# A fixed bank for each kind of transform piece, and a fixed step parity: one change to an FFT filter with a feed-forward layer behind it

## The chip, the cores and the metric

The kernel runs on one core of a Trainium2 chip. A core has five engines with a queue each: TensorE (PE: matmuls, which write to PSUM), VectorE (DVE), ScalarE (ACT), GpSimd (POOL) and SyncE (SP); the last two only issue DMAs here. PSUM is the memory that matmuls write to; this kernel uses it in banks of 128 x 512 float32 values. The metric is the device time of one execution in microseconds (us). The median of the kernel before is 810.01 us over three runs (808.7 to 810.15).

## The reference

```python
def _attn_ref(x, filt_r, filt_i):
    X = np.fft.rfft(x, axis=1)                     # x: (8, 3008, 256)
    F = (filt_r + 1j * filt_i)[None, :, :]         # 1505 frequencies x 256
    y = np.fft.irfft(X * F, n=x.shape[1], axis=1)
    return y.astype(np.float32)

def _moe_ref(x, w_in, w_out, alpha):               # x: (24064, 256), w_in: (256, 2048)
    h = x @ w_in
    g = np.maximum(h, 0.0) + alpha * np.minimum(h, 0.0)
    return (g @ w_out).astype(np.float32)          # w_out: (2048, 256)
```

The second function takes the result of the first, with its 8 sequences laid end to end. Inputs and output are float32.

## The kernel before

**The transform.** A sequence of 3008 = 47 x 64 points is transformed as 47-point transforms, a twiddled 64-point stage, a product with the filter, and the same way back, all as matmuls in float16. For each sequence ("batch", index b = 0 to 7; batch three of the change's name is b = 2) there are four kinds of pieces, each of which fills one PSUM bank and is then read out:

- A (piece_a, line 158; 16 per batch): one 512-column matmul with the 47-point matrix; ScalarE copies it to asb. After every fourth, save_a stores a chunk to memory; turn_a loads all back in another order, as at.
- B (piece_b, line 180; 12): two 256-column matmuls, the forward products. VectorE reads the bank twice: line 188 multiplies by the swapped filter (ww), line 189 by the filter (uu). GpSimd moves the halves of ww across partitions by DMA (sw). piece_s (line 194) adds sw to uu later.
- C (piece_c, line 199; 12): the inverse 64-point stage, two 256-column matmuls (four for b = 1); ScalarE copies it to v. turn_c stores v and loads it back as zt.
- D (piece_d, line 226; 16): four 94-column matmuls, the inverse 47-point stage; ScalarE copies it to yT, the input of the layers.

Batch 0 is done ahead by a class of its own (First), whose transposes (T and piece_t, lines 266 and 303) and D pieces partly reach into the first 47 steps of the main loop; VectorE copies some of them out.

**The layers.** Tokens go through in blocks of 512 (one in twelve has 384). A block has 16 steps. In step j the first layer makes 128 hidden features (up, line 409: two 512-column matmuls); after every odd j ScalarE copies the two halves of a double bank (hps) to gtb (line 420), and VectorE makes the PReLU of it (lines 423 and 424). In the same step the second layer of the block before does its share (down, line 427: four 256-column matmuls; three after a 384-token block). After j = 7 and j = 15 (10 and 15 after a 384-token block) ScalarE copies a finished output to osb (line 438), which SP stores.

**The order.** There are 768 steps. The program is in the order in which it is written out: in each step first the transform pieces that plan (lines 442 to 485) puts there, in the order in which they were put, then up, then down. Each engine goes through its queue in that order. plan_fft gives for b of 3 and over, with p = 96 (b - 1): A at p - 68 + int(2.4 i), B at p + 5 + {0, 4, 10, 14, 20, 24, 30, 34, 40, 44, 50, 54}, the add 8 steps after B, C 12 after B, and D at p + 91, 92, 93, 94, 95, 97, 99 ... 117. So B, the add and C are on odd steps, A on steps of both parities, D from the fifth piece on odd steps. A of batch b + 1 runs in the same steps as B and C of batch b, D of batch b together with B and the first C of b + 1. For b = 2, A is at 66, 68 ... 96, B at 109, 113, 117, 121, 127 ..., C 12 later, D at 187 on. For b = 1, A is at 16 to 31, B at 40, 43 ... 73, C 6 steps after B and ahead of the B of its step, and D at 92 to 96, 98, 100 ... 118.

**The banks.** Of eight banks, four are hps (two double banks), two op (second layer), and two belong to the pool psF, from which A, B, C and D take theirs (bank, line 142; for some pieces of batch 0 a half of hps). A piece's first matmul waits until the earlier piece in that bank has been read. Which of the two banks a piece gets is settled when the program is built.

Of the kernel before, what the change touches and what calls it, by code (L numbers as in the profile page):

```python
# [11 lines left out]
FP32 = mybir.dt.float32  # L12
# [52 lines left out]
def kernel(  # L65
# [27 lines left out]
    p_osb = ctx.enter_context(tc.tile_pool(name="p_osb", bufs=3))  # L93
    psH = ctx.enter_context(tc.tile_pool(name="psH", bufs=2, space=bass.MemoryType.PSUM))
    psO = ctx.enter_context(tc.tile_pool(name="psO", bufs=2, space=bass.MemoryType.PSUM))
    psF = ctx.enter_context(tc.tile_pool(name="psF", bufs=2, space=bass.MemoryType.PSUM))
    dram = ctx.enter_context(tc.tile_pool(name="dram", bufs=1, space=bass.MemoryType.DRAM))
    a_dram = dram.tile([NB, 96, NH, D], FP16, name="a_dram")
    v_dram = dram.tile([NB, 96, NH, D], FP16, name="v_dram")
# [21 lines left out]
    def xrow(b, h, c):  # L121
        return bass.AP(tensor=x.tensor, offset=x.offset + (b * NFFT + NH * h + 8 * c) * D,
                       ap=[[N2 * D, N1], [1, 8 * D]])

    def load_x(b, c):
        xs = p_x.tile([2 * N1, 8 * D], FP16, name="xs")
        for h in range(2):
            nc.gpsimd.dma_start(out=xs[h * N1 : h * N1 + N1], in_=xrow(b, h, c))  # L128
        return xs
# [9 lines left out]
            in_=bass.AP(tensor=src.tensor, offset=src.offset + (N1 - ka) * D,  # L139
                        ap=[[47 * D, 32], [-D, n], [1, D]]))  # L140

    def bank(wide=False):
        if wide:
            return psH.tile([128, 2, 512], FP32, name="hps")[:, 0]
        return psF.tile([128, 512], FP32, name="psF")


    class Fft:
        def __init__(self, b):
            self.b = b  # L150
            self.base = (b % 2) * NFFT
            self.px, self.uw = {}, {}

        def start_a(self):
            self.asb = p_fft.tile([96, NH, D], FP16, name="asb")
            self.at = p_fft.tile([128, NK1, D], FP16, name="at")

        def piece_a(self, i, evict, wide=False):
            if i == 0:
                self.start_a()  # L160
            xs = xc[(self.b, i // 4)]
            ps = bank(wide)
            o = (i % 4) * 512
            nc.tensor.matmul(ps[0:96], wf1_s, xs[:, o : o + 512], start=True, stop=True)  # L164
            evict(self.asb[:, 2 * i : 2 * i + 2].rearrange("p a d -> p (a d)"), ps[0:96])
# [12 lines left out]
                        in_=a_dram[self.b, r + ka : r + kb].rearrange("k s d -> s k d"))  # L178

        def piece_b(self, kp):  # L180
            px = bank().rearrange("p (k d) -> p k d", k=2)
            for kh in range(2):
                k1 = 2 * kp + kh
                nc.tensor.matmul(px[:, kh], twf_s[:, k1], self.at[:, k1], start=True, stop=True)  # L184
            uu = p_uw.tile([128, 2, D], FP16, name="uu", bufs=4)
            ww = p_uw.tile([128, 2, D], FP16, name="ww")
            sw = p_uw.tile([128, 2, D], FP16, name="sw")
            nc.vector.tensor_mul(ww, px, filts_s[:, 2 * kp : 2 * kp + 2])  # L188
            nc.vector.tensor_mul(uu, px, filt_s[:, 2 * kp : 2 * kp + 2])  # L189
            for o in (0, 64):  # L190
                nc.gpsimd.dma_start(out=sw[o : o + 64], in_=ww[64 - o : 128 - o])  # L191
            self.uw[kp] = uu, sw
# [6 lines left out]
        def piece_c(self, kp, evict, pv=None):  # L199
            if kp == 0:  # L200
                self.v = p_fft.tile([128, NK1, D], FP16, name="v")
                self.zt = p_fft.tile([96, NH, D], FP16, name="zt")
            us = self.uw.pop(kp)
            if pv is None:
                pv = bank().rearrange("p (k d) -> p k d", k=2)
            for kh in range(2):
                k1 = 2 * kp + kh
                for u in us:
                    nc.tensor.matmul(pv[:, kh], twi_s[:, k1], u[:, kh], start=u is us[0], stop=u is us[-1])  # L209
            evict(self.v[:, 2 * kp : 2 * kp + 2], pv)  # L210
# [14 lines left out]

        def piece_d(self, i, evict, wide=False):
            g, dh, mh = i // 4, (i // 2) % 2, i % 2
            pd = bank(wide)
            ps = pd[:, 0 : 8 * N1].rearrange("p (m x) -> p m x", m=4)
            for m in range(4):  # L230
                nc.tensor.matmul(ps[:, m], self.zt[:, 8 * g + 4 * mh + m, dh * 128 : dh * 128 + 128],  # L231
                                 wi3_s, start=True, stop=True)
            t0 = self.base + g * 752
            evict(yT[:, dh, t0 : t0 + 752].rearrange("p (x m) -> p x m", m=8)[:, :, 4 * mh : 4 * mh + 4],
                  ps.rearrange("p m x -> p x m"))
# [208 lines left out]
    def put(step, fn, *args):  # L444
        plan.setdefault(step, []).append((fn, args))

    def plan_fft(b, a0, ga, ta, b0, gap, add, lag, d0, quarters, x_at):
        f = Fft(b)
        for i in range(16):
            put(int(a0 + ga * i), f.piece_a, i, on_act)  # L450
        for c in range(4):
            put(int(a0 + ga * (4 * c + 3)), f.save_a, c)
            if b + 1 < NB:
                put(x_at[c],
                    lambda b=b, c=c: xc.update({(b + 1, c): load_x(b + 1, c)}))
        for q in range(quarters):
            w = NK1 // quarters
            put(ta, f.turn_a, nc.sync, w * q, w * q + w)
        bs = [b0 + (2 * int(gap * kp / 2) if add else int(gap * kp)) for kp in range(12)]
        for kp in range(12):  # L460
            put(bs[kp], f.piece_b, kp)
            if add:
                put(bs[kp] + add, f.piece_s, kp)
            put(bs[kp] + lag, f.piece_c, kp, on_act)
        for q in range(4):
            put(bs[3 * q + 2] + lag + 1, f.turn_c, q)
        for i in range(16):
            put(d0 + min(i, 4) + 2 * max(i - 4, 0), f.piece_d, i, on_act)

    for g, t0, d0, gap, evs in ((1, 0, 6, 1, both), (2, 17, 25, 2, (on_dve,)), (3, 32, 40, 2, (on_act,))):  # L470
        for i in range(4):
# [6 lines left out]
    for i in range(4):  # L478
        put(17 + 3 * i, neg, 6 * i, 6 * i + 6)
    put(29, lambda: nc.gpsimd.dma_start(out=filt_s[64:128], in_=filt_s[0:64]))  # L480
    plan_fft(1, 16, 1, 32, 40, 3, 0, 6, 92, 4, (20, 24, 74, 75))
    plan_fft(2, 66, 2, 97, 109, 4.5, 8, 12, 187, 4, (110, 114, 118, 122))
    for b in range(3, NB):
        p = 96 * (b - 1)
        plan_fft(b, p - 68, 2.4, p - 27, p + 5, 5, 8, 12, p + 91, 1, (p + 6, p + 10, p + 16, p + 20))
# [46 lines left out]
```

## Time and profile before

| | us |
|---|---|
| median of three runs | 810.01 |
| profiled execution, first to last instruction (span) | 805.5 |
| TensorE matmuls busy | 781.5 (97%) |
| VectorE busy | 647.0 (80%) |
| ScalarE busy | 599.1 (74%) |
| A: 112 matmuls of 512 columns, of b = 1 to 7 | 43.1 |
| D: 504 matmuls of 94 columns into psF | 41.9 |
| B: 168 matmuls of 256 columns, of b = 1 to 7 | 32.1 |
| ScalarE copy of A, mean | 0.591 |
| ScalarE copy of C, mean | 0.597 |
| ScalarE copy of D, mean | 0.485 |
| ScalarE copy of 128x1024 to gtb, mean | 1.022 |
| VectorE reads of B, mean each | 0.684 and 0.682 |

The page gives no time for the profiled execution beyond its span. In lines of the profile, out<-in are names of the program (psF is any piece's bank), a bracket at the end of a line of the timeline is the idle time of that engine before the instruction and what ended it, and in the view of waits the three numbers are the sum in us, how many, and the longest. Matmuls overlap, and their ends are modelled: two in a row start closer together than either lasts, so the distance of their starts is the measure of TensorE's pace.

### The profile page before, as it was taken

The numbers are of one execution on the slowest core, as the hardware profiler recorded it, in microseconds if no ns is written. First come the engines' busy times: TensorE is split into PE (matmuls) and PEld (weight loads), VectorE is DVE, ScalarE is ACT, GpSimd is POOL, SyncE is SP. The second block draws the span as 40 slices with busy tenths as digits, with TensorE's granted clock in tenths as the row PEclk, the third lists the DMA queues.
The fourth block names the chain that finished last, engine by engine and source line by source line (L and its number), as shares of the span: only waits on it lengthen the run. The fifth ranks groups of instructions, "written<-read, shape, count | busy, mean of one in ns | idle before, by whom it ended". The sixth has DMA issues, their size and how long they took to land.

```text
span 805.5 us, 16163 instructions
## 1 busy us (share of the span) xinstructions
PE 781.5 (97%) x5980; PEld 538.6 (67%) x5980; DVE 647.0 (80%) x1449; ACT 599.1 (74%) x836; POOL 140.4 (17%) x269
## 2 busy tenths in 40 slices
PE   6999999999999999999999999999999999999997
PEld 5756666666666666766667666766666666776665
DVE  4797985899879897798878888798877999777773
ACT  3788677878778777877868877787877867696663
POOL 7410330232004220131102321032200222000000
PEclk9999999999999999999999999999999999999999
DMA  9977457674756446574484543854465233511111
GB/s 187 199 146 207 106 133 176 185 153 120 166 135 125 110 128 149 138 142 112 112 200 99 113 126 104 211 110 112 114 160 141 53 97 85 134 40 34 41 40 53
DMA packets 94247, 100.59 MB, mean 125 GB/s; under 512 B 11320, under 2 KB 81992, under 8 KB 94040
## 3 DMA queue, kind: packets, MB, share of 16 engines
q1 hardware_dynamic: 79512, 68.80, 32.3%
q0 software_dynamic: 14656, 30.75, 20.1%
q8 instruction: 47, 0.77, 0.4%
q14 instruction: 32, 0.26, 0.1%
HBM read 56.26 MB, written 46.66 MB: 128 GB/s over the span
## 4 chain that ended last, share of the span: by engine, by line
PE 74%; DVE 12%; ACT 7%; issue 3%; DMA 3%; SPq 1%; POOL 0%; ACTq 0%; DVEq 0%; POOLq 0%
PE op L433 32%; PE hps L414 31%; ACT gtb L420 4%; DVE m L423 4%; DVE gtb L424 3%; PE psF L209 3%; PE psF L164 2%; DVE ww L188 2%; DVE uu L189 2%; PE psF L231 2%; PE psF L184 1%; ACT asb L238 1%; DMA xs<-in_x_dram 1%; DMA v_dram<-v 1%; ACT osb L438 1%
## 5 line engine op out<-in xcount | busy, mean ns | idle before, releaser
L420 ACT ACTIVATE gtb<-hps 128x1024 f16<-128x1024 f32 (+1 forms) x384 | 385.4, 1004 | 111.2 <-PE hps L414 110.6
L433 PE MATMUL op<-wout_s,gtb 128*128 128x256 f16 x3008 | 451.1, 272 | 0.6 <-DVE gtb L424 0.6
L414 PE MATMUL hps<-yT,win_s 128*128 128x512 f16 (+1 forms) x1536 | 449.1, 374 | 0.4 <-ACT gtb L420 0.2
L433 PEld LDWEIGHTS <-gtb 128*128 128x128 f16 x3008 | 293.3, 98 | 189.5 <-DVE gtb L424 0.9
L423 DVE TENSOR_SCALAR m<-gtb,alm_s 128x512 f16<-128x512 f16 (+1 forms) x768 | 237.7, 351 | 108.1 <-ACT gtb L420 107.3
L424 DVE TENSOR_TENSOR gtb<-gtb,m 128x1024 f16<-128x1024 f16 (+1 forms) x384 | 261.6, 681 | 24.3 <-PE hps L414 0.5
L191 POOL DMA_DIRECT2D sw<-ww x168 | 87.7, 527 | 503.1 <-DVE ww L188 494.1
L414 PEld LDWEIGHTS <-win_s 128*128 128x128 f16 x1536 | 146.1, 98 | 31.1 <-issue 3.1
L238 ACT ACTIVATE yT<-psF 128x376 f16<-128x376 f32 x120 | 58.2, 485 | 25.4 <-PE psF L231 25.1
L238 ACT ACTIVATE asb<-psF 96x512 f16<-96x512 f32 x112 | 66.1, 591 | 12.4 <-PE psF L164 12.0
L238 ACT ACTIVATE v<-psF 128x512 f16<-128x512 f32 x84 | 50.2, 597 | 29.3 <-PE psF L209 28.9
L438 ACT ACTIVATE osb<-op 128x512 f32<-128x512 f32 x96 | 56.3, 586 | 6.1 <-issue 3.2
L188 DVE TENSOR_TENSOR ww<-psF,filts_s 128x512 f16<-128x512 f32 x84 | 57.4, 684 | 0.1
L189 DVE TENSOR_TENSOR uu<-psF,filt_s 128x512 f16<-128x512 f32 x84 | 57.2, 682 | 0.0
L164 PE MATMUL psF<-xs,wf_s 94*96 94x512 f16 x112 | 43.1, 385 | 1.7 <-ACT v L238 1.0
L231 PE MATMUL psF<-wi_s,zt 96*128 96x94 f16 x504 | 41.9, 204 | 2.5 <-DMA zt<-v_dram 1.6
L231 PEld LDWEIGHTS <-zt 96*128 96x128 f16 x512 | 35.4, 97 | 7.3 <-DMA zt<-v_dram 1.9
L128 POOL DMA_DIRECT2D xs<-in_x_dram x64 | 34.8, 555 | 25.6 <-PE psF L164 13.3
L209 PE MATMUL psF<-uu,twi_s 128*128 128x256 f16 x168 | 33.7, 274 | 4.9 <-DVE uu L189 4.5
L184 PE MATMUL psF<-at,twf_s 128*128 128x256 f16 x168 | 32.1, 272 | 0.2
L196 DVE TENSOR_TENSOR uu<-uu,sw 128x512 f16<-128x512 f16 x72 | 30.1, 418 | 0.0
L209 PEld LDWEIGHTS <-twi_s 128*128 128x128 f16 x192 | 16.7, 98 | 12.8 <-DVE uu L189 10.2
(57 smaller groups left out, 191.3 us busy)
## 6 DMA issues: line engine op xcount, KB each, us to landing
out_dram<-osb SPq DMA_DIRECT2D x128, 128.0 KB
xs<-in_x_dram POOLq DMA_DIRECT2D x64, 188.0 KB, 4.4
a_dram<-asb SPq DMA_DIRECT2D x28, 384.0 KB
sw<-ww POOLq DMA_DIRECT2D x168, 64.0 KB, 2.1
v_dram<-v SPq DMA_DIRECT2D x112, 96.0 KB
zt<-v_dram SPq DMA_DIRECT2D x28, 384.0 KB
at<-a_dram SPq DMA_DIRECT2D x20, 384.0 KB
at<-a_dram SPq DMA_DIRECT2D x32, 96.0 KB
```

Of the source, the lines that this page charges most:

```text
L188: nc.vector.tensor_mul(ww, px, filts_s[:, 2 * kp : 2 * kp + 2])
L189: nc.vector.tensor_mul(uu, px, filt_s[:, 2 * kp : 2 * kp + 2])
L191: nc.gpsimd.dma_start(out=sw[o : o + 64], in_=ww[64 - o : 128 - o])
L209: nc.tensor.matmul(pv[:, kh], twi_s[:, k1], u[:, kh], start=u is us[0], stop=u is us[-1])
L231: nc.tensor.matmul(ps[:, m], self.zt[:, 8 * g + 4 * mh + m, dh * 128 : dh * 128 + 128], wi3_s, start=True, stop=True)
L238: nc.scalar.activation(o, i, AF.Copy)
L414: nc.tensor.matmul(self.hps[:, j % 2, 0:tn], win_s[:, kt, j * 128 : (j + 1) * 128], yT[:, kt, self.t0 : self.t0 + tn], start=(kt == 0), st ...
L420: nc.scalar.activation(g[:, :, 0:tn], self.hps[:, :, 0:tn], AF.Copy)
L423: nc.vector.tensor_scalar(m[:, i, 0:tn], g[:, i, 0:tn], 0.0, a, OP.min, OP.mult)
L424: nc.vector.tensor_add(g[:, :, 0:tn], g[:, :, 0:tn], m[:, :, 0:tn])
L433: nc.tensor.matmul(self.op[:, si % 2], self.gts[k][:, 128 * si : 128 * si + 128], wout_s[:, k], start=(k == 0), stop=(k == 15))
L438: nc.scalar.activation(osb[:, 0:m], self.op[:, 0:m], AF.Copy)
```

## The change

The pool psF becomes two pools of one bank each, and bank takes a number. For b of 2 and over, A, C and D always take bank 0 and B bank 1. For b = 0 and 1 a counter flips at each call, and the pieces take the banks strictly in turn. In the plan, A of b of 2 and over goes to even steps only: for b of 3 and over the pieces at offsets 7, 9, 19, 21, 31 and 33 come one step earlier, and so does the first save_a; b = 2 already was on even steps, and for b of 3 and over the others stay. D of b of 2 and over has its pieces 4 to 15 one step later, on even steps (p + 96, 98 ... 118). For b = 1 the plan is as it was. In the diff, the four changed calls of bank are, in order, those of A, B, C and D.

```diff
-    psF = ctx.enter_context(tc.tile_pool(name="psF", bufs=2, space=bass.MemoryType.PSUM))
+    psF = [ctx.enter_context(tc.tile_pool(name=f"psF{i}", bufs=1, space=bass.MemoryType.PSUM)) for i in range(2)]
...
-    def bank(wide=False):
+    side = [0]
+
+    def bank(wide=False, n=None):
         if wide:
             return psH.tile([128, 2, 512], FP32, name="hps")[:, 0]
-        return psF.tile([128, 512], FP32, name="psF")
+        if n is None:
+            side[0] ^= 1
+            n = side[0]
+        return psF[n].tile([128, 512], FP32, name="psF")
...
             self.px, self.uw = {}, {}
+            self.n = (0, 1) if b > 1 else (None, None)
...
-            ps = bank(wide)
+            ps = bank(wide, self.n[0])
...
-            px = bank().rearrange("p (k d) -> p k d", k=2)
+            px = bank(False, self.n[1]).rearrange("p (k d) -> p k d", k=2)
...
-                pv = bank().rearrange("p (k d) -> p k d", k=2)
+                pv = bank(False, self.n[0]).rearrange("p (k d) -> p k d", k=2)
...
-            pd = bank(wide)
+            pd = bank(wide, self.n[0])
...
+        at_a = (lambda i: int(a0 + ga * i)) if b == 1 else (lambda i: 2 * int((a0 + ga * i) / 2))
         for i in range(16):
-            put(int(a0 + ga * i), f.piece_a, i, on_act)
+            put(at_a(i), f.piece_a, i, on_act)
         for c in range(4):
-            put(int(a0 + ga * (4 * c + 3)), f.save_a, c)
+            put(at_a(4 * c + 3), f.save_a, c)
...
+        at_d = 4 if b == 1 else 3
...
-            put(d0 + min(i, 4) + 2 * max(i - 4, 0), f.piece_d, i, on_act)
+            put(d0 + min(i, at_d) + 2 * max(i - at_d, 0), f.piece_d, i, on_act)
```

## The prediction

> **What bounds the kernel now.** I read the page first, then the view of who waited for whom, then the timeline around the places that the change touches.
>
> ```profile
> span 805.5 us, 16163 instructions
> PE 781.5 (97%) x5980; PEld 538.6 (67%) x5980; DVE 647.0 (80%) x1449; ACT 599.1 (74%) x836; POOL 140.4 (17%) x269
> PEclk9999999999999999999999999999999999999999
> PE 74%; DVE 12%; ACT 7%; issue 3%; DMA 3%; SPq 1%; POOL 0%; ACTq 0%; DVEq 0%; POOLq 0%
> ```
>
> TensorE is the bound and its clock is full throughout. In the timeline its matmuls start back to back: 216 ns apart at 512 columns, 109 at 256, 41 at 94; a step without transform pieces takes 2 x 216 + 4 x 109 = 868 ns. So what counts is lost starts: the distance of two starts less the streaming time of the first. Added up over the timeline from 90 us on they are 15.9 us. So I count what each bank change adds or removes there. No other engine is near 100% over a long stretch, and a wait of TensorE moves everything behind it.
>
> ```profile
> PE psF L209 <- DVE uu L189: 4.5, 15, 0.8
> PE psF L231 <- DMA zt<-v_dram: 1.6, 1, 1.6
> PE psF L164 <- ACT v L238: 1.0, 2, 0.5
> ```
>
> Inverse pieces (C, line 209) wait 15 times for line 189, VectorE's second read of a forward product (B): the C piece got the bank that B still held. That is what the change takes away. (This view counts idle time from modelled ends, so it reads lower than the lost starts.)
>
> ```profile
> 203.03 0.60 ACT L238 ACTIVATE v<-psF 128x512 f16<-128x512 f32 x1 [0.45 <-PE psF L209]
> ...
> 203.68 0.38 PE L164 MATMUL psF<-xs,wf_s 94*96 94x512 f16 x1 [0.47 <-ACT v L238]
> ```
>
> This row gives the price of sharing a bank with ScalarE: the next user starts 0.05 us after the copy's end.
>
> **Steps 209 to 637 and later (b = 3 to 7): C.** Lost starts of C, and of A behind C in the same step, are in the timeline 2.20, 2.87, 2.20, 2.86 and 0.57 us for b = 3 to 7: 10.7 us (this includes 0.04 us on each first-layer matmul behind a C-A pair). All vanish. But C now shares bank 0 with A and D, and these now sit on even steps, just ahead of C's odd ones. The case is in the trace:
>
> ```profile
> 277.45 1.02 ACT L420 ACTIVATE gtb<-hps 128x1024 f16<-128x1024 f32 x1 [0.81 <-PE hps L414]
> ...
> 277.69 0.38 PE L164 MATMUL psF<-xs,wf_s 94*96 94x512 f16 x1
> ...
> 278.37 0.59 ACT L438 ACTIVATE osb<-op 128x512 f32<-128x512 f32 x1
> 278.54 0.68 DVE L189 TENSOR_TENSOR uu<-psF,filt_s 128x512 f16<-128x512 f32 x1
> 278.85 0.59 ACT L238 ACTIVATE asb<-psF 96x512 f16<-96x512 f32 x1
> ...
> 279.28 0.39 PE L209 MATMUL psF<-uu,twi_s 128*128 128x256 f16 x2 [0.34 <-DVE uu L189]
> ```
>
> Step 232 runs A at 277.69; ScalarE copies it at 278.85 to 279.44, since the gtb copy of the odd step before and an output copy stand ahead. C of step 233 could start at 277.69 + 1.09 = 278.78, waits for VectorE until 279.28 (0.50), and on A's bank would wait until 279.49: 0.71. Without an output copy (steps 222 and 223) A's copy ends at 267.97, C could start at 267.80: 0.22, where VectorE cost 0.34. Behind D the copy is shorter: 0.16, or 0.63 behind an output copy (0.43 where that is the half-size one, after the 384-token block). From the new plan, with p = 96(b-1), C of p+17 and p+21 come behind D (the first with an output copy), p+31, 37, 47, 61 behind A, p+41 and 57 behind A with an output copy, and p+27, 51, 67, 71 behind an empty step. Sum per batch: 0.63 + 0.16 + 4 x 0.22 + 2 x 0.71 = 3.07 (2.87 for b = 4, 6); b = 7 has only D, 0.79. In all 12.7 for 10.7: +2.0. A behind C waits nothing: C's copy ends 1.05 us after C's start, the next step comes at 1.09, and this margin is thin.
>
> **D of b = 2 to 7.** Its first four steps stay consecutive, and now on one bank: in the trace the third would wait 0.17 us for the copy of the second (b = 2, 4, 6) or 0.11 (3, 5, 7): +0.84. The 12 others (4 matmuls and a copy each, no DMA) move one step later; the first block that reads them starts ten steps after, so nothing waits.
>
> **C of b = 2** (steps 121 to 169): now 1.52 of lost starts; then C behind A at 125, 133, 139, 143, 151, 157 for 0.22 each and 129, 161 with an output copy for 0.71: 2.73. +1.2.
>
> **Moved A** (six per batch b = 3 to 7: one matmul and one copy each, one step earlier, and with the fourth the save_a store of chunk 0): on the SP queue no other issue stands between old and new step, POOL gets none; nothing.
>
> **Batches b = 0 and 1: strict turns.** Before, one pool had both banks, and a piece got the one that came free first:
>
> ```profile
> 50.83 0.38 PE L164 MATMUL psF<-xs,wf_s 94*96 94x512 f16 x1
> ...
> 51.64 0.68 DVE L241 CAST zt<-psF 96x512 f16<-96x512 f32 x1
> ```
>
> A of step 18 started at 50.83, while the bank of step 17's transpose was read until 52.32: it took the other. The new code flips a side at each call, so it must take this one: 52.36, a wait of 1.53. By going on like this in the timeline, letting VectorE run on while TensorE waits: step 20 waits 0.05 (VectorE has caught up), step 22 1.00, step 28 0.97, step 32 0.26; waits of 0.28, 0.28 and 0.11 (steps 19, 21, 29) go. Steps 16 to 32: +3.1.
>
> From step 40 on, counting flips, B of b = 1 always has side 0 and C side 1, and A of b = 2 (bank 0, steps 66 to 96) runs into B:
>
> ```profile
> 111.91 0.38 PE L184 MATMUL psF<-at,twf_s 128*128 128x256 f16 x2
> ...
> 112.80 0.38 PE L164 MATMUL psF<-xs,wf_s 94*96 94x512 f16 x1 [0.51 <-ACT v L238]
> ...
> 114.16 0.68 DVE L189 TENSOR_TENSOR uu<-psF,filt_s 128x512 f16<-128x512 f32 x1
> ```
>
> In step 70 A would follow B at 112.13, waits now until 112.80 (0.67), and on B's bank until 114.89: 2.75. Likewise A of step 66 waits for B of 64 (read until 107.88; A at 106.91): 1.02; A of 68 for B of 67: 0.65 (B's reads end 1.70 us after its start when VectorE is free, the next A comes 1.09 after); A of 74: 0.66; C of 79 behind A of 78: 0.23. B of 73 keeps its 0.28. Steps 66 to 80: 1.02 + 0.65 + 2.08 + 0.66 + 0.23 = +4.6. VectorE's reads are what is late there: a step-69 copy and three VectorE instructions stand ahead of B's, so the wait moves on whole.
>
> Steps 92 to 118 (D of b = 1 in turns, A of b = 2 on bank 0, B of b = 2 on bank 1): D at 93, 95, 98 behind A's copies 0.23, 0.37, 0.10; B at 109, 113, 117 behind D's copies 0.48, 0.55, 0.17; a wait of 0.18 at 112 goes: +1.7. The 1.8 us that D's first piece waits for its zt load stays: that chain starts from C of step 79 and moves with it.
>
> **Sum**: 2.0 + 0.8 + 1.2 + 3.1 + 4.6 + 1.7 = +13.4 us, on the profiled span 805.5: 818.9. The page gives no time around the span; the median of the timed runs is 810.0, 4.5 above it, and I keep that: 823.4.
>
> **The clock.** Longest new wait: 2.75 us. The present one of 1.8 us at 136.64 left the granted clock at 1.00 from 134 to 140 us, so I put nothing. The Trainium skill (TensorE: Matmul & The Clock Gate, "A second HAM failure mode: psum-queue depth-cycling") says that waiting on PSUM banks between groups of matmuls can make the clock swing between half and full. This trace, with its 15.9 us of lost starts at a full clock, does not bear it out; if it held, the sum would be that of rival 3.
>
> **Bounds.** The waits on ScalarE are read from copies that are in the trace; what is not there is how far an engine catches up while TensorE waits. If VectorE doesn't catch up, steps 18 to 32 cost what their present lags say, 1.53 + 1.29 + 1.07 + 0.54 + 0.97 + 0.35 + 0.26 less the 0.67 that goes, 5.3 for 3.1, and A of 68 0.90 for 0.65: with the thin margin of A behind C (some 35 pairs, at most 0.05 us each), up to +18, 828. If it catches up more, steps 16 to 80 cost half: +9.5, 819.5.
>
> **Rivals.** (1) The early part does not come: the first two batches' pieces still find the bank that is free, as before. For it: before did so; against it: two pools of one bank each and a counter leave no choice. Then 2.0 + 0.8 + 1.2 = +4.0: 814.0. (2) Faster: ScalarE's copies are not late. If A's copy began within 0.45 us of A's start (1.09 less 0.59 less 0.05) C would never wait; then the 12.2 us of b = 2 to 7 go, the ScalarE waits of steps 79 to 118 and of D don't come, and the VectorE waits 3.1 + 4.4 stay: -4.7, 805.3. Against it: on even steps of the 512-token blocks A's copies begin 0.68 us after A, 1.16 with an output copy, behind the gtb copy, whose place doesn't change. (3) The clock drops after the 2.75 us wait. The trace's own half-clock stretch is its start: 128-column matmuls 107 ns apart from 2.67 to 5.4 us, 56 after. One such stretch of 2.7 us loses 1.4 us: 824.8. (4) The two effects cancel, within 0.2% (1.6 us, about what these runs can tell from no change).
>
> **How the numbers follow.** Forecast as summed, with its bounds 819.5 to 828: 0.75. (1) 0.11, (3) 0.03: slower together 0.89. (2) 0.08. (4) 0.03. Range: 812.5 to 828 takes in the forecast and (1) and (3), leaving out about one in ten.
>
> **What would show it** (line numbers of the kernel before). Right: the row of line 209 waiting for DVE uu goes, line 209 waiting for ACT asb (and yT) comes, some 40 times, 0.2 or 0.7 us each; line 164 waits for DVE uu and zt, a few times, 1 to 2.75 us, before 120 us; TensorE's starts from 209 on lose about 13.5 us in place of 10.7. Wrong: no wait of line 164 over 1 us before 120 us (rival 1), or line 209 starting 1.09 us after A throughout (rival 2).

## The result and the profile after

The changed kernel takes 823.06 us (median of four runs, 822.31 to 824.32); the kernel before, beside it on the same chip, takes 809.36 (808.09 to 810.15, four runs). The ratio is 1.0178 (95% interval 1.016 to 1.0196): slower by 13.7 us, where the prediction said 823.4 in a range of 812.5 to 828. The profiled execution of the changed kernel took 823.26 us with a span of 821.5, so 1.8 us lie around the span.

The page of the changed kernel: span, engines, the clock that TensorE was granted, and the shares of the chain that ended last.

```profile
span 821.5 us, 16161 instructions
PE 786.9 (96%) x5980; PEld 541.5 (66%) x5980; DVE 647.8 (79%) x1449; ACT 595.1 (72%) x836; POOL 139.9 (17%) x269
...
PEclk9999999999999999999999999999999999999999
...
PE 80%; ACT 9%; DVE 5%; issue 2%; DMA 2%; POOL 0%; SPq 0%; ACTq 0%; DVEq 0%; POOLq 0%
```

TensorE does the same 5980 matmuls. In the chain, VectorE's share has gone from 12% to 5% and ScalarE's from 7% to 9%: the waits for VectorE's reads went, and waits for ScalarE's copies came. The view of waits (sum in us, how many, the longest) says at which pieces. Lines are moved by 6 against the kernel before: 170 is A, 190 B, 195 VectorE's second read of B, 215 C, 237 D, 244 a ScalarE copy, 247 a VectorE copy.

```profile
PE psF L170 <- DVE uu L195: 4.5, 4, 2.6
PE psF L215 <- ACT asb L244: 4.4, 8, 0.6
...
PE psF L215 <- ACT yT L244: 2.3, 5, 0.5
PE psF L170 <- DVE zt L247: 1.8, 2, 1.0
PE psF L237 <- DVE yT L247: 1.4, 1, 1.4
```

The row of C waiting for uu is gone. In its place C waits for ScalarE's copies of A (asb) and of D (yT), and four A of b = 2 (the row with uu) wait for VectorE: the banks of the early steps. This view counts only what the modelled ends leave over; counted as lost starts, as in the prediction, C waits 42 times from 140 us on, for 16.2 us. Here are two of them in the timeline, at step 229 (without an output copy) and step 233 (with one):

```profile
286.21 1.02 ACT L426 ACTIVATE gtb<-hps 128x1024 f16<-128x1024 f32 x1 [0.67 <-PE hps L420]
...
286.45 0.38 PE L170 MATMUL psF<-xs,wf_s 94*96 94x512 f16 x1
286.96 0.68 DVE L195 TENSOR_TENSOR uu<-psF,filt_s 128x512 f16<-128x512 f32 x1
287.13 0.58 ACT L244 ACTIVATE asb<-psF 96x512 f16<-96x512 f32 x1
...
287.77 0.38 PE L215 MATMUL psF<-uu,twi_s 128*128 128x256 f16 x2
```

```profile
290.81 0.38 PE L170 MATMUL psF<-xs,wf_s 94*96 94x512 f16 x1
291.49 0.59 ACT L444 ACTIVATE osb<-op 128x512 f32<-128x512 f32 x1
...
291.97 0.59 ACT L244 ACTIVATE asb<-psF 96x512 f16<-96x512 f32 x1
292.61 0.38 PE L215 MATMUL psF<-uu,twi_s 128*128 128x256 f16 x2 [0.55 <-ACT asb L244]
```

In the first, C could have started 1.09 us after A, at 287.54; it starts at 287.77, 0.05 after ScalarE has emptied A's bank, and 0.23 is lost. In the second the output copy stands ahead of A's copy: 0.72 lost.

**Where the 13.7 us are.** For each step the timeline gives the start of its first-layer matmul; the difference to the same step of the kernel before, and where that difference grows, is the account of the change. The profiled execution of the changed kernel is one column; a second profiled execution of the same kernel, from the experiments (span 820.9), is the other. The main loop's first step comes at another time in each execution, 0.9 and 1.4 us later here than in the profile before, and that is left out.

| steps | predicted | first profile | second |
|---|---|---|---|
| 0 to 16 | 0 | 0.72 | 0.72 |
| 16 to 32 | 3.1 | 2.75 | 2.74 |
| 33 to 64 | 0 | -0.33 | -0.23 |
| 64 to 80 | 4.6 | 6.24 | 4.85 |
| 81 to 92, with the zt wait of step 92 | 0 | -0.51 | -0.48 |
| 93 to 118 | 1.7 | 1.73 | 1.75 |
| 118 to 169: C of b = 2 | 1.2 | 1.26 | 1.27 |
| 169 to 767: C and D, b = 3 to 7, and D of b = 2 | 2.8 | 3.23 | 3.32 |
| sum | 13.4 | 15.1 | 13.9 |

The first profile has 1.67 us that the second lacks: TensorE's clock. (The row of steps 64 to 80 differs by 1.4, since B of step 73 then no longer waits its 0.28.) At step 70 A waits for B's bank, 2.76 us by starts, and then:

```profile
117.75 0.38 PE L190 MATMUL psF<-at,twf_s 128*128 128x256 f16 x2
120.73 0.45 PE L170 MATMUL psF<-xs,wf_s 94*96 94x512 f16 x1 [2.60 <-DVE uu L195]
120.99 1.05 PE L420 MATMUL hps<-yT,win_s 128*128 128x512 f16 x2
121.83 1.06 PE L439 MATMUL op<-wout_s,gtb 128*128 128x256 f16 x4
...
124.62 0.59 PE L420 MATMUL hps<-yT,win_s 128*128 128x512 f16 x2
```

First-layer pairs that take 0.59 elsewhere take 1.05 from 120.99 on. In the view by windows (us, then busy time of PE, PEld, DVE, ACT and POOL with the number of instructions, then the granted clock, the share of the DMA engines in use and GB/s) the half clock lasts exactly one stretch of 3.41 us:

```profile
117.60:120.99 3.39, 0.79 (x7) 0.37 (x6) 2.51 (x5) 0.99 (x2) 0.61 (x2) 1.00 0.39 89
120.99:124.40 3.41, 3.41 (x14) 1.87 (x13) 0.00 (x0) 1.22 (x2) 0.42 (x1) 0.50 0.29 65
```

### The profile page after: what moved, and what is told of

The parts are those of the page before. It is cut to its first block, busy times and chain, and to the rows that moved or that the text cites. A ratio compares the mean times of both kernels' runs of the same rounds, so it can differ in the third digit from the quotient of the medians.

```text
span 821.5 us, 16161 instructions
## 1 busy us (share of the span) xinstructions
PE 786.9 (96%) x5980; PEld 541.5 (66%) x5980; DVE 647.8 (79%) x1449; ACT 595.1 (72%) x836; POOL 139.9 (17%) x269
## 4 chain that ended last, share of the span: by engine, by line
PE 80%; ACT 9%; DVE 5%; issue 2%; DMA 2%; POOL 0%; SPq 0%; ACTq 0%; DVEq 0%; POOLq 0%
PE hps L420 35%; PE op L439 34%; ACT gtb L426 5%; PE psF L215 3%; PE psF L237 2%; ACT asb L244 2%; PE psF L190 2%; PE psF L170 2%; DVE m L429 1%; ACT osb L444 1%; DVE gtb L430 1%; DMA xs<-in_x_dram 1%; PE hps L287 1%; DVE ww L194 1%; ACT yT L244 0%
## 5 line engine op out<-in xcount | busy, mean ns | idle before, releaser
L420 PEld LDWEIGHTS <-win_s 128*128 128x128 f16 x1536 | 144.1, 98 | 32.5 <-issue 4.9
L215 PEld LDWEIGHTS <-twi_s 128*128 128x128 f16 x192 | 18.6, 97 | 19.2 <-issue 16.9
```

The source lines that it names most:

```text
L420: nc.tensor.matmul(self.hps[:, j % 2, 0:tn], win_s[:, kt, j * 128 : (j + 1) * 128], yT[:, kt, self.t0 : self.t0 + tn], start=(kt == 0), st ...
```

## The experiments

The prediction's theory: a bank of its own takes the wait on VectorE from C, and puts C, A and D behind ScalarE's queue and the early pieces behind B's reads; nothing else matters. Each experiment takes out one part of that.

**1. One step of the long wait.**

```diff
-            put(at_a(i), f.piece_a, i, on_act)
+            put(at_a(i) + (b == 2 and i == 2), f.piece_a, i, on_act)
```

> The changed kernel, with one A piece of b = 2 (the third, step 70, the one that waited 2.76 us behind B of its own step) put one step later, at 71. Its wait for VectorE's second read ends at the same moment, so by the bank alone the kernel gains the one step that TensorE now does in that time: 0.87 us, 822.2. Theory (the half clock from 120.99 to 124.40 us in the changed kernel's records follows from the 2.76 us without a matmul): the wait is now 1.89 us, about the 1.8 us that the kernel before stood without a drop, no half-clock stretch follows, and the 1.7 us that it cost go too: 820.5. Rival (the drop comes at some moment of its own): a half-clock stretch of 3.4 us stays somewhere between 100 and 140 us, 822.2.

820.7 us (820.34 to 823.51), 1.015 of before. A's wait is 1.89 us in place of 2.76, and the clock stays full. By the account above the steps behind the start hold 13.0 us, 0.9 to 1.0 less than the second profile of the changed kernel, which is the shorter wait; the rest of the 2.4 us is a start of the main loop that came 1.3 us earlier in this execution. So the wait is B's bank, as said:

```profile
120.19 0.42 PE L170 MATMUL psF<-xs,wf_s 94*96 94x512 f16 x1 [1.73 <-DVE uu L195]
```

That the time came out at the expected 820.5 is luck: the expectation counted 1.7 us for the clock, and the earlier start stood in for it. On the clock the run says nothing, as experiment 5 shows.

**2. Banks alone, with the steps of before.**

```diff
-        at_a = (lambda i: int(a0 + ga * i)) if b == 1 else (lambda i: 2 * int((a0 + ga * i) / 2))
+        at_a = lambda i: int(a0 + ga * i)
...
-        at_d = 4 if b == 1 else 3
+        at_d = 4
```

> The changed kernel's banks with the steps of the kernel before (A on both parities, D on odd steps). Theory (what costs is ScalarE's copy of the piece just before in bank 0): A behind C in the same step now waits for C's copy, 0.84 us each, C behind D in the same step 0.73, and C behind A on an even step 0.22 or 0.71 as before. From the copies' ends in the trace of the kernel before: 5.6 us a batch for b = 3 to 6, 1.5 for b = 7, 4.4 for b = 2, 1.7 for five D in a row; 30.0 in place of 17.1 in the changed kernel: 836. Rival (the parity matters little, the early batches carry the loss): within 1 us of 823.

837.17 us (835.75 to 838.39), 1.0346. Its view of waits:

```profile
PE psF L170 <- ACT v L244: 10.1, 15, 0.7
PE psF L215 <- ACT yT L244: 5.7, 10, 0.6
PE psF L170 <- DVE uu L195: 4.5, 4, 2.6
PE psF L215 <- ACT asb L244: 3.9, 7, 0.6
```

Where A stands in the same step as C, behind it on the same bank, it waits 15 times by starts, 14 of them for 0.85 us, and C behind D waits 7.3 us in place of 4.0. The moved steps, whose worth the prediction never summed, save 14 us once the banks are as they are.

**3. Steps alone, with the shared pool of before.**

```diff
-    psF = [ctx.enter_context(tc.tile_pool(name=f"psF{i}", bufs=1, space=bass.MemoryType.PSUM)) for i in range(2)]
+    psF = ctx.enter_context(tc.tile_pool(name="psF", bufs=2, space=bass.MemoryType.PSUM))
...
-        return psF[n].tile([128, 512], FP32, name="psF")
+        return psF.tile([128, 512], FP32, name="psF")
```

> The changed kernel's steps (A and D on even steps) with the one pool of two banks of the kernel before. Theory (the loss comes from the fixed banks): no loss over 1 us before step 120, since the early pieces find the free bank again; C still waits for VectorE's second read of B in most places, 0.3 to 0.5 us, and A behind C in one step (0.15 to 0.21 and 0.04 behind it) goes: between 807 and 812. Rival (the moved steps themselves cost, by crowding ScalarE): over 815.

807.16 us (805.71 to 809.16), 0.9981 of before (0.9967 to 0.9995): faster by 0.2%, just measurable. So all of the loss is the banks'. C's waits for VectorE are still there, and no wait of A for uu in the early steps (212 is C here, 192 the read of B):

```profile
PE psF L212 <- DVE uu L192: 3.4, 11, 0.8
```

**4. Banks of b = 0 and 1 by reader instead of strictly in turn.** A takes bank 0 and B bank 1; for C, D and the transposes T a fixed rule by their number names the bank that its last reader has left by then. Only the first eight T and D of b = 0 still take turns.

```diff
-            ps = bank(wide, self.n[0])
+            ps = bank(wide, 0)
...
-            px = bank(False, self.n[1]).rearrange("p (k d) -> p k d", k=2)
+            px = bank(False, 1).rearrange("p (k d) -> p k d", k=2)
...
-                pv = bank(False, self.n[0]).rearrange("p (k d) -> p k d", k=2)
+                pv = bank(False, int(self.b == 1 and kp > 9)).rearrange("p (k d) -> p k d", k=2)
...
-            pd = bank(wide, self.n[0])
+            pd = bank(wide, (None, int(i < 10), 0)[min(self.b, 2)] if self.b or i < 8 else int(i < 12))
...
-            pt = bank(wide)
+            pt = bank(wide, None if i < 8 else int(i < 12))
```

> The changed kernel, with b = 0 and 1 no longer in strict turns from step 16 on: what VectorE reads (transposes and D of steps 17 to 31, B) on bank 1, what ScalarE reads on bank 0, and the last two C and first ten D of b = 1 on bank 1, away from A of b = 2. Theory (strict turns put A behind VectorE's reads): A no longer waits over 0.7 us before 120 us, no half-clock stretch, and of the 10.1 us that steps 16 to 118 cost more than in the kernel before, all but about 0.5 go: 813.5 (812.5 to 814.5), 4 to 5 above the kernel before, which is the ScalarE waits of b = 2 to 7. Rival (early waits come from elsewhere, the order of loads or ScalarE): over 818.

812.95 us (812.25 to 813.51), 1.0047: 10.1 us less than the changed kernel. Steps 16 to 118 add in sum 0.0 us to the kernel before where the strict turns add 8.6 (second profile); the other 1.4 of the 10.1 are an earlier start of the main loop in this execution. The rows of line 170 on uu and zt are gone, and these stay:

```profile
PE psF L215 <- ACT asb L244: 6.1, 11, 0.6
PE psF L215 <- ACT yT L244: 3.2, 6, 0.9
PE psF L237 <- DVE yT L247: 1.4, 1, 1.4
```

That is the late part, 1.26 for b = 2 and 3.3 for b = 3 to 7, and 0.71 at step 9, where turns are still taken. This splits the loss much as the prediction did: two thirds, 9.4 of the 13.9 us by the account, come from the strict turns of the first two batches.

**5. The clock.** The changed kernel again, and with 42 small matmuls on the identity (an existing helper; nobody reads their result) to keep TensorE streaming in the wait.

```diff
+    put(70, warm, 42)
     plan_fft(2, 66, 2, 97, 109, 4.5, 8, 12, 187, 4, (110, 114, 118, 122))
```

> The changed kernel once more, on the chip of the next three. Theory (the clock is granted in stretches of 3.41 us, and a stretch in which TensorE mostly waits brings half the clock in the next; the records of five profiles agree): whether the 2.76 us wait of step 70 brings a drop depends on where it falls in that raster, so a drop of one stretch (1.7 us) behind it may be there or not; 821.4 without and 823.1 with it. Rival: the wait always brings it.

> The changed kernel with 42 small matmuls (128 columns, 56 ns each, 2.35 us) of an identity, into a bank of the second layer, ahead of A of step 70, so that TensorE works in the 2.76 us that it waited; nothing else moves. Theory (the half clock follows from TensorE standing still, not from the wait as such): A starts at the same moment as in the changed kernel, no half-clock stretch between 115 and 130 us in any profile, 821.4, like the repeated run without its drop. Rival (the drop has another cause): 823.1 and a half-clock stretch at the same place.

823.05 us (822.71 to 823.98) for the unchanged kernel and 823.88 (823.39 to 826.04) for the filled one. The unchanged kernel's profile has the same 2.13 us more at step 70 and no half clock behind it. In windows of 3.41 us that lie as the clock's stretches do in this execution, the wait falls into two of them:

```profile
116.92:120.33 3.41, 1.82 (x15) 1.19 (x13) 2.08 (x5) 1.57 (x3) 0.00 (x0) 1.00 0.15 35
120.33:123.74 3.41, 2.40 (x15) 1.52 (x16) 0.95 (x2) 1.24 (x2) 1.04 (x2) 1.00 0.60 138
```

Experiment 1 had expected a drop that follows from the wait as such. That fell: it comes in one execution and not in another. The number expected for the repeated run fell all the same: 821.4 without a drop, where this execution without one took 822.71. It began its main loop 0.5 us later than the first, and B of step 73 waited its 0.28 again. The filled kernel kept its clock at step 70, which then proves nothing, and lost it elsewhere, behind the wait for D's first piece in step 92 (D's groups of four take 0.47 and 0.52 us at 147.53 and 149.28, and 0.33 otherwise):

```profile
146.13 0.34 PE L237 MATMUL psF<-wi_s,zt 96*128 96x94 f16 x4 [2.27 <-DMA zt<-v_dram]
147.53 0.47 PE L237 MATMUL psF<-wi_s,zt 96*128 96x94 f16 x4
149.28 0.52 PE L237 MATMUL psF<-wi_s,zt 96*128 96x94 f16 x4
151.19 0.33 PE L237 MATMUL psF<-wi_s,zt 96*128 96x94 f16 x4
```

That wait was 2.27 there and 1.03 in the unchanged kernel's second profile: the four stores of v ahead of the zt load took SP 3.57 us in place of 2.34. By the account the longer wait costs 1.2 us and the half clock another 1.2 in this execution. The expectation for the filled kernel missed by 2.5 us, but 1.7 of them it shares with the unchanged one; the medians of the two differ by 0.8. Why the stores took longer stays open.

**6. The output copy out of the way.** Output copy and store are put behind the next step's transform pieces.

```diff
+    late = []
...
-                    osb = p_osb.tile([128, 2, D], FP32, name="osb")
-                    nc.scalar.activation(osb[:, 0:m], self.op[:, 0:m], AF.Copy)
-                    for lane in range(m):
-                        store(self.p, self.t0 + 128 * (si - m + 1 + lane), osb, lane)
+                    def copy_out(op=self.op, m=m, si=si):
+                        osb = p_osb.tile([128, 2, D], FP32, name="osb")
+                        nc.scalar.activation(osb[:, 0:m], op[:, 0:m], AF.Copy)
+                        for lane in range(m):
+                            store(self.p, self.t0 + 128 * (si - m + 1 + lane), osb, lane)
+                    late.append(copy_out)
...
             for fn, args in plan.pop(step, ()):
                 fn(*args)
+            while late:
+                late.pop(0)()
             blk.up(j)
```

> The changed kernel with ScalarE's copy of a finished second-layer output (and its store) put behind the transform pieces of the next step, and so behind ScalarE's copy of A or D. Theory (C waits for the copy of the A or D just ahead of it in bank 0, and that copy for what stands ahead in ScalarE's queue): the ten waits of 0.72 us become 0.23, the five of 0.56 to 0.66 behind D 0.18, B behind D at 109 and a few before lose some 0.5: 7.1 to 8 us in all, 815.5. Rival (the waits come from the bank alone or from PSUM, not from the order on ScalarE): within 1 us of the repeated run.

813.99 us (811.96 to 817.51), 9.1 less than the changed kernel beside it, though this execution has a half-clock stretch behind step 70 again (121.84 to 125.26). Every C that lost 0.72 behind an output copy now loses 0.23, and each C behind D 0.18 (0.28 in two places): from step 169 on the loss against before turns from +3.3 to -2.6. Step 233 again, with the output copy now behind A's (446 is the output copy here):

```profile
287.74 0.38 PE L170 MATMUL psF<-xs,wf_s 94*96 94x512 f16 x1
288.42 0.59 ACT L244 ACTIVATE asb<-psF 96x512 f16<-96x512 f32 x1
...
288.90 0.60 ACT L446 ACTIVATE osb<-op 128x512 f32<-128x512 f32 x1
289.06 0.38 PE L215 MATMUL psF<-uu,twi_s 128*128 128x256 f16 x2
```

That shows what the 0.72 are made of. But it is not all the bank's, as the same edit on the kernel before shows:

> The kernel before, with the output copy and its store put behind the transform pieces of the next step, as in e6_output_copy_later. Theory (the 9 us that this gave the changed kernel are its own waits on ScalarE's copies; before has hardly any, and its C pieces wait for VectorE's reads): no change, 807.5 to 809, the waits of line 209 on uu stay. Rival (the later output copy is worth something by itself, so that e6_output_copy_later measured that and not the bank): 799 to 801.

804.51 us (803.22 to 806.09), 0.9957 (0.9942 to 0.9973). Neither expectation held: 3.5 us are to be had in the kernel before, too. 1.8 of them are the zt wait of step 92. SP's queue in the kernel before, and with the later output copy (x is the number of DMAs):

```profile
125.74 2.33 SPq L396 DMA_DIRECT2D out_dram<-osb  x3
128.12 2.35 SPq L218 DMA_DIRECT2D v_dram<-v  x4
132.19 2.63 SPq L224 DMA_DIRECT2D zt<-v_dram  x4
```

```profile
125.97 2.36 SPq L218 DMA_DIRECT2D v_dram<-v  x4
130.00 1.72 SPq L224 DMA_DIRECT2D zt<-v_dram  x4
```

Three stores of finished outputs stood ahead of the stores of v that zt is loaded from; without them zt is issued 2.2 us earlier, though the main loop of this execution runs 1.6 us later there, and D's first piece doesn't wait. The rest is 1.1 us at steps 25, 46 and 73, and 0.28 at each of four C pieces (step 233 and its like in the next three batches), whose wait falls from 0.50 to 0.23.

**7. Steps that no reader contests.** If the mechanism is right, C's waits go when no piece stands on bank 0 just ahead of it. On the kernel of experiment 4, A and D of b = 2 and later go to even steps that aren't followed by a C, as far as there are such, the first four D two steps apart; and D of step 9 no longer takes its turn behind VectorE.

```diff
-            pd = bank(wide, (None, int(i < 10), 0)[min(self.b, 2)] if self.b or i < 8 else int(i < 12))
+            pd = bank(wide, (None, int(i < 10), 0)[min(self.b, 2)] if self.b else (None if i < 7 else int(i < 12)))
...
+        p = 96 * (b - 2)
-        at_a = (lambda i: int(a0 + ga * i)) if b == 1 else (lambda i: 2 * int((a0 + ga * i) / 2))
+        at_a = {1: range(16, 32), 2: range(66, 98, 2),
+                3: (122, 124, 126, 130, 132, 134, 136, 138, 140, 144, 148, 152, 154, 158, 162, 166)}.get(
+            b, [p + x for x in (30, 32, 34, 36, 38, 42, 44, 46, 48, 50, 52, 54, 58, 62, 64, 68)])
+        at_d = [92, 93, 94, 95] + [96 + 2 * x for x in range(12)] if b == 1 else [
+            p + 96 + x for x in (88, 90, 92, 94, 96, 98, 100, 102, 104, 106, 108, 110, 114, 118, 120, 124)]
...
-        plan_fft(b, p - 68, 2.4, p - 27, p + 5, 5, 8, 12, p + 91, 1, (p + 6, p + 10, p + 16, p + 20))
+        plan_fft(b, p - 68, 2.4, p - 27 + 3 * (b == 3), p + 5, 5, 8, 12, p + 91, 1, (p + 6, p + 10, p + 16, p + 20))
```

> The kernel with banks by reader (812.95), with A and D of b = 2 and over on even steps that are not just ahead of a C, as far as there are such steps (three A a batch still are, none with an output copy ahead), the first four D two steps apart, and for batch 0 the D of step 9 in the bank that ScalarE frees. Theory: of the ScalarE waits of b = 2 to 7 (2.8, 3.2, 3.1, 3.2, 3.1 and 0.8 us, and 0.9 behind consecutive D) all but 0.7 a batch go, and 0.7 of step 9: 298 steps later nothing else takes their place, 799 (798 to 801), about 10 below the kernel before. Rival (another engine then becomes late, VectorE first, with 80% busy): 803 or more.

820.75 us (819.0 to 820.95), a miss by over 20. C's waits had gone as meant, and another row had come:

```profile
PE psF L237 <- DMA zt<-v_dram: 14.3, 6, 3.9
```

D's first piece stood three steps earlier than before, and its zt load had not landed; behind two of these waits the clock was halved as well (235.25 to 238.66 and 334.23 to 341.06). So the first four D went back, on two banks by turns:

```diff
-            pd = bank(wide, (None, int(i < 10), 0)[min(self.b, 2)] if self.b else (None if i < 7 else int(i < 12)))
+            pd = bank(wide, (None, int(i < 10), int(i in (1, 3)))[min(self.b, 2)] if self.b else (None if i < 7 else int(i < 12)))
...
-            p + 96 + x for x in (88, 90, 92, 94, 96, 98, 100, 102, 104, 106, 108, 110, 114, 118, 120, 124)]
+            p + 96 + x for x in (91, 92, 93, 94, 96, 98, 100, 102, 104, 106, 108, 110, 114, 118, 120, 124)]
```

> The kernel of e7_free_steps with one thing more: the first four D of each batch from b = 2 on are back at steps 91 to 94 of their batch, on the two banks by turns; the other twelve stay on even steps that are not ahead of a C. Theory (what e7_free_steps lost is the zt load that D's first piece reached too early, with the half clock behind two of those waits; what it did at the C pieces was right): the waits of D's first piece for zt, 3.9, 3.6, 1.8, 2.2 and 2.1 us, go, no half clock after 140 us, and what is left are a dozen waits of C of 0.23 us; in e7_free_steps the lost time of C fell by 0.9 us in b = 2 and by 1.2 to 2 in each of b = 3 to 7, 8 to 9 in all, against before: 799.5 (798 to 801), 8 below before. Rival (moving A and D to other steps costs by itself, by ScalarE's copies falling due at other places, and the zt wait only showed it first): at or above before, 807 to 812, with waits of TensorE from 180 us on that are neither zt nor C's 0.23.

804.56 us (802.95 to 806.43), 0.9951 (0.9936 to 0.9966): faster than before, but by under half of what was expected. Beside that of step 92 two zt waits were left, 2.47 us at 233.88 and 1.45 at 329.91, and SP's queue shows the first. First the kernel before, then this one:

```profile
212.52 2.25 SPq L176 DMA_DIRECT2D at<-a_dram  x4
...
218.17 2.09 SPq L218 DMA_DIRECT2D v_dram<-v  x4
223.41 1.73 SPq L224 DMA_DIRECT2D zt<-v_dram  x4
```

```profile
218.31 2.76 SPq L182 DMA_DIRECT2D at<-a_dram  x4
221.11 3.24 SPq L224 DMA_DIRECT2D v_dram<-v  x4
230.07 1.73 SPq L230 DMA_DIRECT2D zt<-v_dram  x4
```

The moved A had pushed the load of at to right before the stores of v, and zt was issued 6.7 us later, 0.6 of them because the main loop of this execution runs later there. The last of the v stores left SP 4.1 us later; why zt then followed 5.7 us behind it and not 3.2 as in the kernel before, these rows don't show. The next kernel lets the last A end no later than before, and puts D's fifth and sixth pieces on steps 95 and 96, the sixth on bank 1:

```diff
-            pd = bank(wide, (None, int(i < 10), int(i in (1, 3)))[min(self.b, 2)] if self.b else (None if i < 7 else int(i < 12)))
+            pd = bank(wide, (None, int(i < 10), int(i in (1, 3, 5)))[min(self.b, 2)] if self.b else (None if i < 7 else int(i < 12)))
...
-                3: (122, 124, 126, 130, 132, 134, 136, 138, 140, 144, 148, 152, 154, 158, 162, 166)}.get(
-            b, [p + x for x in (30, 32, 34, 36, 38, 42, 44, 46, 48, 50, 52, 54, 58, 62, 64, 68)])
+                3: (122, 124, 126, 130, 132, 134, 136, 138, 140, 142, 144, 146, 148, 152, 154, 158)}.get(
+            b, [p + x for x in (28, 30, 32, 34, 36, 38, 42, 44, 46, 48, 50, 52, 54, 58, 62, 64)])
...
-            p + 96 + x for x in (91, 92, 93, 94, 96, 98, 100, 102, 104, 106, 108, 110, 114, 118, 120, 124)]
+            p + 96 + x for x in (91, 92, 93, 94, 95, 96, 98, 100, 102, 104, 106, 108, 110, 114, 118, 120)]
...
-        plan_fft(b, p - 68, 2.4, p - 27 + 3 * (b == 3), p + 5, 5, 8, 12, p + 91, 1, (p + 6, p + 10, p + 16, p + 20))
+        plan_fft(b, p - 68, 2.4, p - 27, p + 5, 5, 8, 12, p + 91, 1, (p + 6, p + 10, p + 16, p + 20))
```

> The kernel of e8_four_d_back, in which the trace shows the zt load of batch two issued on SP's queue at 230.07 where before issues it at 223.41: the at load of batch three stood at 218.31 instead of 212.52, close ahead of the stores of v that zt waits for, since A of the next batch ended later there. Here the last A is at most as late as in before (step 158 for b = 3, p + 64 from b = 4 on), the at load is back on the step of before, and D's fifth and sixth pieces take steps 95 and 96 on the two banks so that step 28 of the next batch is free for A. Theory (two zt waits, 2.47 and 1.45, were all that kept it from the expected time): both go, and what is left in b = 2 to 7 are waits of C of 0.23 us, some four a batch: 800.5 (799 to 802), 8 below before. Rival (zt waits also for something else, a VectorE or ScalarE copy that the new steps push back): the waits behind 230 us stay, 804 to 805 as in e8_four_d_back.

799.74 us (799.29 to 800.07), 0.988 of before (0.9859 to 0.9901). The chain's shares by engine, and the view of waits:

```profile
PE 87%; ACT 6%; DVE 3%; DMA 2%; issue 1%; SPq 0%; POOL 0%; ACTq 0%; DVEq 0%; POOLq 0%
```

```profile
PE psF L237 <- DMA zt<-v_dram: 1.1, 1, 1.1
...
PE psF L215 <- ACT yT L244: 0.9, 1, 0.9
...
PE psF L215 <- ACT asb L244: 0.6, 1, 0.6
```

TensorE holds 87% of the chain, 74% before. One zt wait is left, that of step 92. The two C rows are one wait each, of b = 1 (85 and 117 us); what is left from 168 us on are 21 waits of C of 0.23 us by starts, too short for this view. With the output copy of experiment 6 on top:

> e10_at_load_back with the output copy and its store behind the next step's transform pieces, which took 3.6 us off before, 1.8 of them the zt wait of step 92, the rest at pieces that wait for a ScalarE copy behind an output copy. Theory (the first of these goes here too, since batch one's D steps are the same; of the second there is next to nothing left to win): 1.5 to 2.5 below e10_at_load_back, 798 to 799. Rival (the two gains are the same time): as e10_at_load_back, within 0.5.

798.22 us (796.85 to 799.07), 0.9862 of before (0.9842 to 0.9882): 1.5 less, and the zt wait of step 92 is gone (1.3 less there). So fixed banks, which cost 1.8% as the change was written, stand in a kernel that is 1.2% faster than before once few pieces stand ahead of C on the shared bank and the early batches don't take turns blindly; the later output copy adds 0.2%, and it gives 0.4% to the kernel before as well. Two things stay open. Bank 1 is no longer for forward products alone: three D of each later batch use it, and ten D and two C of b = 1. And no run has these steps with the shared pool, so how much of the 1.2% is the banks' and how much the steps' isn't shown.

The Trainium skill advises to rotate independent matmul groups through different banks, so that the read-out of one overlaps the matmuls of the next (Perfetto Trace Analysis, "Optimizing Tensor Performance", Matmuls). These runs bear it out in part: on the steps of the change the shared pair (807.16) beats the fixed banks (823.06), but strict turns are a rotation too, and by the account they took 8.7 us more than banks by reader (experiment 4). What decided here is which reader was late.

## Why the prediction was right

**In place and size, mostly.** The forecast of 823.4 against 823.06 rests on a sum of +13.4 us against 13.9 in the second profile.

- *C of b = 3 to 7*: the row of C on uu went and that of asb and yT came, some 40 times. Predicted 0.22 behind A and 0.71 with an output copy, measured 0.230 and 0.717; behind D 0.16 and 0.63, measured 0.175 and 0.664; with the half-size output copy 0.43, measured 0.56. The C waits of b = 3 to 7 come to 13.4 us, 12.7 predicted: 0.7 more, where that row of the table is 0.4 to 0.5 above the prediction; the other 0.3 went in differences under 0.03 us each. A behind C waits nothing, as said; D's third piece waits 0.88 us in all for 0.84.
- *C of b = 2* and *steps 93 to 118*: 1.26 for 1.2 and 1.73 for 1.7.
- *Steps 16 to 32*: 2.75 for 3.1. A of step 18 lost 1.12 instead of 1.53: VectorE was less late than reckoned, perhaps since the wait of step 9 (below) had let it catch up.
- *Steps 64 to 80 without the clock*: 4.85 for 4.6. A of 66 1.06, of 68 0.71, of 70 2.13 more than before, of 74 0.71, C of 79 0.23. Experiment 4 shows the cause of all of these and of steps 16 to 32 and 93 to 118: with the banks fixed by reader A of 66, 68 and 74 no longer waits, A of 70 waits as before the change, and the three stretches together add nothing (64 to 80 still 0.67, where C of 67 and 73 now waits for ScalarE).
- *Rival 1* (the early part does not come, 814.0) describes what experiment 4 made: 812.95. *Rival 2* (faster, since ScalarE's copies are not late) did not come: C stands 1.09 us behind A nowhere on the shared bank, 1.32 or 1.81 instead. Its idea, that C without these waits makes the kernel faster, is what experiment 7 ends with.

**What it had wrong.**

- *"Steps 16 to 32" begins too late.* In strict turns D of step 9 takes the bank that VectorE's copy of step 7 still holds, 0.72 us, in every kernel with the turns there (the row of line 237 on DVE yT, 1.4). The prediction went through the turns from step 18 only.
- *"4.5 above the span, and I keep that".* The page gave no time around the span; the profiles of the runs here put it at 1.8 us. The other 2.7 were not around the span: the profiled execution was one of the quicker ones (runs of before have spans of 804.9 to 809.5). The profiles of these kernels differ in when the main loop begins, 37.1 to 40.8 us, 37.6 in that of before; whether that is also what sets runs of before apart isn't shown, as only one of them has a profile. That the sum came within 0.4 us of the median is luck in this term.
- *"The clock: I put nothing."* The first profile has the stretch, for 1.67 us, where rival 3 had priced 1.4; the second has none, and the medians of both sets of runs are equal. The row of 1.8 us at full clock was read as if length alone decided. In the changed kernel the clock stays at 1.00 over some forty waits of 0.2 to 0.7 us for a bank, and drops behind one wait of 2.76 us in one of its two profiles. The Trainium skill (TensorE: Matmul & The Clock Gate, "A second HAM failure mode: psum-queue depth-cycling") tells of frequent short stops of TensorE between groups of matmuls that make the clock swing; the trace does not agree for the forty waits, and a drop behind a single long wait is not what that section describes.
- *"The 1.8 us of D's first piece stays"*: it fell to 1.18 by starts, 0.6 less; the chain of stores and loads did not move with C as a whole.

## What to carry over

When pieces get fixed banks, look for each bank at who empties it: the next user pays for as long as that reader's queue is late, here 0.23 us behind one ScalarE copy and 0.72 with another ahead of it, so here a bank set apart for one reader went with a gain only on steps on which the others were on time. A counter that flips does not replace a choice of bank by reader: by the account that alone was 8.7 us. A piece that is moved by a few steps takes its DMAs along, and a load that went 6.7 us later on SP's queue went with a wait of 2.47 us, ten bank waits' worth.

## What was not expected of the hardware

**The clock changes on a raster of 3.41 us.** Every half-clock stretch that lies within a trace is one or more times 3.41 us long (121.84 to 125.26, 235.25 to 238.66, 147.41 to 150.83; 334.23 to 341.06 is two). In windows laid on that raster, the share of the window ahead in which TensorE streamed (columns of its matmuls at full clock) was 0.18 in the changed kernel, 0.33 in experiment 6, 0.34 in the filled kernel, 0.11 and 0.18 in experiment 7; where it was 0.45 (experiment 1, a wait of 1.89 us), 0.47 (the kernel with four D back, behind its wait of 2.47 us) and 0.48 (the second profile), the clock stayed. So a wait of 2.4 to 2.8 us costs nothing more, or 1.2 to 1.7 us more; by these shares that goes by where it falls in the raster. In the first 24 us of some executions stretches also followed windows with shares of 0.40 to 0.59, so a share between 0.34 and 0.45 as the bound is a reading of these few cases, not a rule. The Trainium skill has the raster (TensorE: Matmul & The Clock Gate, "What's actually happening": a free-running window of 3413 ns) and the trace agrees on its length; that page speaks of an idle window, and here windows with a third of their time in use were enough.

**A bank is handed on in 0.05 us.** From the end of the read that a matmul waited for to the start of that matmul the traces have 0.049 to 0.053 us behind ScalarE's copies and 0.052 to 0.058 behind VectorE's reads, whatever the wait was. In the row of 287.77 above it is 0.051. The prediction had read 0.05 from one row, and its prices behind ScalarE came out within 0.04 us but for the half-size output copy (0.43 predicted, 0.56 measured).
